# Fewer and earlier tap transfers, and half a cast moved to GpSimd, in a fused causal convolution and gated feed-forward kernel

## The chip, the cores and the metric

The kernel runs on one core of a Trainium2 chip. The core has a matrix engine (TensorE, PE in the profile), a vector engine (VectorE, DVE), an activation engine (ScalarE, ACT), a general engine (GpSimd, POOL) and SyncE (SP), which here only issues DMA transfers. POOL and ACT issue DMA transfers too. All engines run their own instruction lists in order and wait for each other by semaphores. The metric is the device time of one execution in microseconds (us); the median over several runs counts.

## The reference

`x` has shape (8, 4096, 192): 8 batches of 4096 tokens with 192 channels. `weight` is (8, 7): 8 heads of 24 channels each, 7 taps for each head. The taps of a head go through a softmax, and each channel of a token becomes the weighted sum of the last 7 tokens of its batch. The result goes through a gated feed-forward net with 1536 hidden columns.

```
w = exp(weight - max(weight)); w = w / (sum(w) + 1e-9)
y[b, s, h, g] = sum_k w[h, k] * x_pad[b, s + k, h, g]      # 6 zero tokens ahead of each batch
out = (relu(y @ w_gate) * (y @ w_val)) @ w_out
```

All inputs and the output are float32; the kernel works in float16 with float32 sums.

## The kernel before

**Units.** The tokens are cut into 16 units. A unit holds 1024 tokens of two batches, four batches apart, which are called streams; stream 0 lies on partitions 0 to 63 and stream 1 on 64 to 127 of the tile `xc` (channels in three chunks of 64, tokens along the row). `gate_val(u, w)` makes, for each of two windows of 512 tokens and each of 12 hidden blocks `f`, the gate and the value matmuls (line 530), ScalarE's relu (line 539) and VectorE's product (line 540). `project_columns` then multiplies with `Wo` (line 550) in three parts `p` = 0, 1, 2, and VectorE's `turn_out` (line 564) takes each part out of PSUM. PSUM is one ring of four double banks named `ps`, shared by all of these in program order.

**Two ways to the convolution.** For units 0 and 1 the convolution is done by TensorE with banded matrices (`conv_dense`, line 334, for unit 0 and the first window of data after it, and `conv`, line 356, whose results ScalarE copies out at line 369 and SyncE's DMA transposes bring into `xc[1]` at line 388). From unit 2 on it is done by the other engines while TensorE works on an earlier unit: `lane_load` fetches x, `lane_turn` reorders it on POOL (lines 433 and 439) and has SyncE transpose it with DMAs into the tile `x_r` (lines 434 and 441), `lane_first` (ACT, line 487), `product` (ACT, line 467), `lane_rest` (DVE, line 498 and 508) and `add` (POOL, line 476) multiply the shifted rows with the taps and add them. All of them read the tile `tap`, which has for each of 128 partitions and three chunks the 7 softmax weights of that channel's head.

**The front.** SyncE first issues five loads of float32 x (`load_raw`, line 111), in the order of the steps 1, 0, 2, 3, 4. They are cast to float16 by `cast` (line 121): steps 1, 0 and 2 on ACT, steps 3 and 4 on DVE. POOL makes a few constants (lines 141 to 160) and then issues ten loads of `w_gate` and `w_val` (`load_w`, line 208: five column slices each, cast to float16 on the way), which land on partitions 0 to 63. Copies bring each slice to partitions 64 to 127 too (`both_halves`, line 215): the first two on DVE, the next three on POOL, and the last, columns 1280 to 1535 (hidden blocks 10 and 11), by two DMAs from SyncE. POOL then loads x for `conv_dense(1)` and `conv(2)` (line 94), x for unit 2 (line 402), a 16-token head (line 413) and `Wo` (line 614).

**Taps.** ACT makes the normalized weights `wn` (line 259) on 128 partitions, 16 equal rows for each head. `load_taps` (line 283 and after) first issues the two DMAs of the last weight slice and then copies rows of `wn` to `tap`, at most 16 rows in one DMA: 32 DMAs (line 297). All of these, and the transposes after them, stand in SyncE's one list. Each DMA of SyncE takes the next of eight completion semaphores, and waits till the one eight before it has landed.

The order of the instructions is the program's own: a manual schedule, without a planner.

Of the kernel before, what the change touches and what calls it, by code (L numbers as in the profile page):

```python
# [15 lines left out]
def kernel(  # L16
# [12 lines left out]
    nc = tc.nc  # L29

    B, S, D = x.shape
    H, KW = weight.shape
    G = D // H
# [3 lines left out]
    NCH = D // 64  # L37
# [38 lines left out]
    def staged(i, j):  # L76
        return stages[i][:, XH * j : XH * (j + 1)]

    def load_x(g, streams=range(2)):
# [22 lines left out]
    xts = {0: staged(0, 0).rearrange("p (j s d) -> p j s d", s=2, d=D)}  # L102
    ROWS = [SUB + PAD, 128, 128, 128, 80]
    raw = [
        apool.tile([128, FLAT - LDVE], FP, name=f"prod{jj + 1}")[:, 0 : 2 * D] for jj in range(GSUB)
    ]
# [10 lines left out]
            ),  # L117
        )

    def cast(copy, jj):  # L120
        copy(
            out=xts[0][0 : ROWS[jj], jj, :, :].rearrange("p s d -> p (s d)"),
            in_=raw[jj][0 : ROWS[jj], :],
        )

    HR = 128 // H
# [35 lines left out]
    with nc.allow_low_precision("one of the terms is not zero"):  # L162
        nc.vector.tensor_reduce(
            out=Z[:, 112 : 112 + HR],
            in_=eye[:].rearrange("p (g i) -> p i g", i=HR),
# [4 lines left out]
        out=mask[:, :, 0],  # L170
        in_=eye[:].rearrange("p (g i) -> p g i", i=HR),
# [17 lines left out]
    for half in range(2):  # L189
        nc.tensor.matmul(  # L190
            out=raised[half][:, 0, 0 : SUB * H // 2],
# [7 lines left out]
    Wg = const.tile([128, NCH, DFF], F16)  # L199
    Wv = const.tile([128, NCH, DFF], F16)  # L200
# [4 lines left out]
    def load_w(s):  # L205
        cols = slice(CUTS[s], CUTS[s + 1])
        for src, dst in ((moe_w_gate, Wg), (moe_w_val, Wv)):
            nc.gpsimd.dma_start(
                out=dst[0:64, :, cols],
                in_=src.rearrange("(c p) f -> p c f", p=64)[:, :, cols],  # L210
            )

    def both_halves(copy, s, dst):
        cols = slice(HALVES[s], HALVES[s + 1])
        copy(out=dst[64:128, :, cols], in_=dst[0:64, :, cols])

    def pool_halves(s):
        both_halves(nc.gpsimd.tensor_copy, s, Wg)
        both_halves(nc.gpsimd.tensor_copy, s, Wv)

    for s in range(5):
        load_w(s)
    pool_halves(2)
# [6 lines left out]
        out=mx[:], in_=spread[:, 0, 0:KW], axis=mybir.AxisListType.X, op=ALU.max, negate=True  # L230
    )
    nc.scalar.activation(out=e[:, 0:KW], in_=spread[:, 0, 0:KW], func=ACTF.Exp, bias=mx[:])
    cast(nc.scalar.copy, 1)
    cast(nc.scalar.copy, 0)
    prod = const.tile([128, BW, KW], FP)
    z0 = Z[:, 112 - PAD : 113 - PAD]
    e0 = e[:, 0:1]
    nc.vector.tensor_tensor(
        out=prod[:],
# [11 lines left out]
        out=blocks[:],  # L251
# [6 lines left out]
    wn = const.tile([128, KW], FP)  # L258
    nc.scalar.activation(out=wn[:], in_=e[:, 0:KW], func=ACTF.Copy, scale=sm[:])
    cast(nc.scalar.copy, 2)  # L260

    bands = [const.tile([128, H // 2, SUB], F16, name=f"band{half}") for half in range(2)]
    for half, copy in enumerate((nc.vector.tensor_copy, nc.scalar.copy)):
        for j in range(128 // HR):
            s0 = HR * j - PAD
            lo, hi = max(0, -s0), min(BW, SUB - s0)
            nc.tensor.matmul(
                out=raised[half][:, 0, 0 : SUB * H // 2].rearrange("p (h t) -> p h t", t=SUB)[
                    :, :, s0 + lo : s0 + hi
                ],  # L270
# [7 lines left out]
            out=bands[half][:].rearrange("p h t -> p (h t)"), in_=raised[half][:, 0, 0 : SUB * H // 2]  # L278
# [4 lines left out]

    tap = const.tile([128, NCH, KW], FP)

    def load_taps():
        both_halves(nc.sync.dma_start, 5, Wg)
        both_halves(nc.sync.dma_start, 5, Wv)
        for c in range(NCH):
            r0 = 0  # L290
            while r0 < 64:
                h = (64 * c + r0) // G
                r1 = min(64, G * (h + 1) - 64 * c)
                for st in range(2):
                    for a in range(r0, r1, HR):
                        n = min(HR, r1 - a)
                        nc.sync.dma_start(  # L297
                            out=tap[64 * st + a : 64 * st + a + n, c, :],
                            in_=wn[HR * h : HR * h + n, :],
                        )  # L300
                r0 = r1

    load_taps()

    def band(h):
        return bands[h // 4][0 : SUB + PAD, h % 4, :]
# [383 lines left out]
```

## Time and profile before

| | |
|---|---|
| time, median of 3 runs | 774.67 us (773.52 to 777.39) |
| the profiled execution, its own time | 775.43 us |
| its span from first to last instruction | 773.7 us |
| TensorE busy | 763.6 us, 99% |
| VectorE busy | 669.3 us, 86% |
| ScalarE busy | 598.0 us, 77% |
| GpSimd busy | 422.5 us, 55% |
| mean granted TensorE clock | 0.998 |

A timeline row has the start in us, the length in us (of all merged instructions, if it ends with x and a number above 1), engine, line, operation and tiles; in brackets stands the idle time of that engine before the row and what ended it. "SPq" and "POOLq" are issues of DMAs; a DMA's landing time is counted from its issue. A row of the table by windows has the busy time of each engine in that stretch, the granted clock (PEclk), and the DMA traffic. In the chain of waits each row is a piece of the one chain of work that ended last.

### The profile page before, as it was taken

The numbers are of one execution on the slowest core, as the hardware profiler recorded it, in microseconds if no ns is written. First come the engines' busy times: TensorE is split into PE (matmuls) and PEld (weight loads), VectorE is DVE, ScalarE is ACT, GpSimd is POOL, SyncE is SP. The second block draws the span as 40 slices with busy tenths as digits, with TensorE's granted clock in tenths as the row PEclk, the third lists the DMA queues.
The fourth block names the chain that finished last, engine by engine and source line by source line (L and its number), as shares of the span: only waits on it lengthen the run. The fifth ranks groups of instructions, "written<-read, shape, count | busy, mean of one in ns | idle before, by whom it ended". The sixth has DMA issues, their size and how long they took to land.

```text
span 773.7 us, 21558 instructions
## 1 busy us (share of the span) xinstructions
PE 763.6 (99%) x9402; PEld 380.1 (49%) x9402; DVE 669.3 (86%) x630; ACT 598.0 (77%) x622; POOL 422.5 (55%) x190
## 2 busy tenths in 40 slices
PE   9988999999999999999999999999999999999998
PEld 4543544444444444444444444444444444444448
DVE  6858999989899898998989899898998989997691
ACT  6868787878879788797877879788797877874471
POOL 9405839368292864909458193773918548091000
PEclk9999999999999999999999999999999999999999
DMA  9934909066190842809148090651909332040402
GB/s 146 123 64 92 134 7 163 4 94 71 24 143 2 120 45 57 109 3 140 26 83 83 6 158 5 107 60 34 132 3 122 43 67 59 2 82 3 82 2 83
DMA packets 123438, 53.79 MB, mean 70 GB/s; under 512 B 87872, under 2 KB 123344, under 8 KB 123344
## 3 DMA queue, kind: packets, MB, share of 16 engines
q1 hardware_dynamic: 86416, 38.06, 30.2%
q0 software_dynamic: 36768, 14.26, 17.8%
q8 instruction: 73, 1.20, 0.7%
q14 instruction: 21, 0.17, 0.1%
q10 hardware_dynamic: 160, 0.10, 0.0%
HBM read 29.40 MB, written 25.17 MB: 71 GB/s over the span
## 4 chain that ended last, share of the span: by engine, by line
PE 91%; SPq 3%; ACT 2%; DMA 2%; issue 0%; DVE 0%
PE ps L530 61%; PE ps L550 28%; PE ps L586 2%; SPq L297 2%; ACT prod L467 1%; SPq L441 1%; DMA tap<-wn 1%; DMA prod<-in_x_dram 1%; ACT gr L539 0%; DVE hT L540 0%; DMA x_r<-x_p 0%; ACT out_s L369 0%; ACT acc L487 0%; PE ps L334 0%; SPq L111 0%
## 5 line engine op out<-in xcount | busy, mean ns | idle before, releaser
L539 ACT ACTIVATE gr<-ps 128x1024 f16<-128x1024 f32 x384 | 392.6, 1023 | 148.1 <-PE ps L530 147.7
L540 DVE TENSOR_TENSOR hT<-gr,ps 128x1024 f16<-128x1024 f16 x384 | 468.5, 1221 | 42.4 <-ACT gr L539 15.4
L476 POOL TENSOR_TENSOR prod<-prod,prod 128x1792 f32<-128x1792 f32 x70 | 278.3, 3976 | 262.9 <-DVE prod L508 226.2
L530 PE MATMUL ps<-xc,Wv 64*128 64x512 f16 x2304 | 313.0, 377 | 2.3 <-DVE out_s L564 1.7
L530 PE MATMUL ps<-xc,Wg 64*128 64x512 f16 x2304 | 313.1, 377 | 1.0 <-ACT gr L539 1.0
L550 PE MATMUL ps<-hT,Wo 128*32 128x512 f16 x4320 | 236.2, 379 | 2.2 <-DVE out_s L564 2.2
L530 PEld LDWEIGHTS <-Wv 64*128 64x128 f16 x2304 | 130.7, 94 | 121.4 <-issue 4.2
L530 PEld LDWEIGHTS <-Wg 64*128 64x128 f16 x2304 | 112.2, 94 | 139.3 <-issue 8.6
L550 PEld LDWEIGHTS <-Wo 128*32 128x32 f16 x4320 | 114.4, 97 | 122.4 <-issue 8.8
L467 ACT ACTIVATE prod<-x_r,tap 128x1024 f32<-128x1024 f16 (+1 forms) x182 | 172.8, 1037 | 0.0
L498 DVE SCALAR_TENSOR_TENSOR acc<-x_r,tap,acc 128x1024 f32<-128x1024 f16 (+1 forms) x140 | 113.9, 870 | 8.8 <-DMA xc<-out_s 8.6
L564 DVE STREAM_TRANSPOSE out_s<-ps 128x1024 f32<-128x1024 f32 x45 | 56.1, 1247 | 32.1 <-PE ps L550 32.1
L476 POOL TENSOR_TENSOR xc<-prod,prod 128x1792 f16<-128x1792 f32 x14 | 55.7, 3979 | 1.1
L439 POOL COPY x_p<-x_e 128x1536 f16<-128x1536 f16 x28 | 40.3, 1467 | 2.0 <-DMA x_e<-in_x_dram 2.0
L402 POOL DMA_DIRECT2D x_e<-in_x_dram x28 | 25.0, 900 | 4.2 <-POOL x_p L439 4.2
L487 ACT ACTIVATE acc<-x_r,tap 128x1024 f32<-128x1024 f16 (+1 forms) x28 | 21.5, 819 | 6.7 <-DMA x_r<-x_p 6.7
L498 DVE SCALAR_TENSOR_TENSOR xc<-x_r,tap,acc 128x1024 f16<-128x1024 f16 (+1 forms) x28 | 23.4, 876 | 0.0
L586 PE MATMUL ps<-Wo,hT 128*128 128x192 f16 x192 | 16.0, 246 | 0.0
L586 PEld LDWEIGHTS <-hT 128*128 128x128 f16 x192 | 15.8, 98 | 0.4 <-issue 0.4
L597 ACT COPY out_s<-ps 128x768 f32<-128x768 f32 (+2 forms) x5 | 3.2, 639 | 12.7 <-PE ps L586 12.7
L597 DVE COPY out_s<-ps 128x192 f32<-128x192 f32 x1 | 0.4, 357 | 13.3 <-PE ps L586 13.3
L508 DVE TENSOR_SCALAR prod<-x_r,tap 128x768 f32<-128x768 f16 x14 | 8.5, 610 | 0.0
(55 smaller groups left out, 61.6 us busy)
## 6 DMA issues: line engine op xcount, KB each, us to landing
out_dram<-out_s SPq DMA_DIRECT2D x63, 384.0 KB, 7.5
x_e<-in_x_dram POOLq DMA_DIRECT2D x28, 384.0 KB, 10.3
x_r<-x_p SPq DMA_TRANSPOSE x112, 3.1
out_s<-in_x_dram POOLq DMA_DIRECT2D x4, 240.0 KB, 5.9
prod<-in_x_dram SPq DMA_DIRECT2D x3, 192.0 KB
Wo<-in_moe_w_out_dram POOLq DMA_DIRECT2D x1, 576.0 KB, 10.6
out_s<-in_x_dram POOLq DMA_DIRECT2D x2, 192.0 KB, 4.1
tap<-wn SPq DMA_DIRECT2D x16, 0.4 KB, 3.4
```

Of the source, the lines that this page charges most:

```text
L402: nc.gpsimd.dma_start(out=xe[:, :, st, :, :].rearrange("p j c r -> p j (c r)"), in_=bass.AP(tensor=x.tensor, offset=x.offset + row * D, ap ...
L439: nc.gpsimd.tensor_copy(out=xp[:, :, :, st, :], in_=xe[:, :, st, :, :])
L467: nc.scalar.activation(out=prods[u, k][:, at - LDVE : at - LDVE + n], in_=shifted(u, c, k, t, n), func=ACTF.Copy, scale=tap[:, c, k : k + 1],)
L476: nc.gpsimd.tensor_tensor(out=p0[:] if k < KW - 1 else flat(u)[:, LDVE:FLAT], in0=p0[:], in1=prods.pop((u, k))[:], op=ALU.add,)
L487: nc.scalar.activation(out=accs[u][:, at : at + n], in_=shifted(u, c, 0, t, n), func=ACTF.Copy, scale=tap[:, c, 0:1],)
L498: nc.vector.scalar_tensor_tensor(out=(flat(u) if k == KW - 1 else acc)[:, at : at + n], in0=shifted(u, c, k, t, n), scalar=tap[:, c, k : k ...
L530: nc.tensor.matmul(out=pss[i][:, st, :], lhsT=W[64 * st : 64 * st + 64, c, 128 * f : 128 * (f + 1)], rhs=xcb[64 * st : 64 * st + 64, c, WI ...
L539: nc.scalar.activation(out=gr[:], in_=pss[0][:], func=ACTF.Relu)
L540: nc.vector.tensor_tensor(out=h[:, f], in0=gr[:], in1=pss[1][:], op=ALU.mult)
L550: nc.tensor.matmul(out=ps[32 * s : 32 * s + 32, b, :], lhsT=Wo[:, f, 64 * p + 32 * b : 64 * p + 32 * b + 32], rhs=hs[s // 2][:, f, s % 2, ...
L564: nc.vector.transpose(out=o[:, :, 64 * p : 64 * p + 64].rearrange("p t (b c) -> p b t c", b=2), in_=ps[:].rearrange("p b (t c) -> p b t c" ...
L586: nc.tensor.matmul(out=ps[:, i // 2, D * (i % 2) : D * (i % 2) + D], lhsT=h[:, f, st, 128 * q : 128 * (q + 1)], rhs=Wo[:, f, :], start=(f ...
```

## The change

The code of three places differs; the order of everything else is the same.

1. The taps are sent in 20 DMAs instead of 32. One DMA covers all rows of a chunk that belong to one head in one stream (8, 16 or 24 rows), and reads 8 rows of `wn`, each of them one, two or three times by a step of zero.
2. The 14 DMAs of the chunks 0 and 1 stand in SyncE's list ahead of the two DMAs of the last weight slice; the 6 of chunk 2 stand behind them.
3. The cast of x step 1 is split: GpSimd casts the first 192 of the 384 columns before it issues the ten weight loads, and ACT casts the other 192.

```diff
-    def cast(copy, jj):
+    def cast(copy, jj, lo=0, hi=2 * D):
         copy(
-            out=xts[0][0 : ROWS[jj], jj, :, :].rearrange("p s d -> p (s d)"),
-            in_=raw[jj][0 : ROWS[jj], :],
+            out=xts[0][0 : ROWS[jj], jj, :, :].rearrange("p s d -> p (s d)")[:, lo:hi],
+            in_=raw[jj][0 : ROWS[jj], lo:hi],
         )
...
+    cast(nc.gpsimd.tensor_copy, 1, 0, D)
     for s in range(5):
         load_w(s)
...
-    cast(nc.scalar.copy, 1)
+    cast(nc.scalar.copy, 1, D)
     cast(nc.scalar.copy, 0)
...
-    def load_taps():
-        both_halves(nc.sync.dma_start, 5, Wg)
-        both_halves(nc.sync.dma_start, 5, Wv)
-        for c in range(NCH):
-            r0 = 0
-            while r0 < 64:
-                h = (64 * c + r0) // G
-                r1 = min(64, G * (h + 1) - 64 * c)
-                for st in range(2):
-                    for a in range(r0, r1, HR):
-                        n = min(HR, r1 - a)
-                        nc.sync.dma_start(
-                            out=tap[64 * st + a : 64 * st + a + n, c, :],
-                            in_=wn[HR * h : HR * h + n, :],
-                        )
-                r0 = r1
-
-    load_taps()
+    for c in range(NCH):
+        r0 = 0
+        while r0 < 64:
+            h = (64 * c + r0) // G
+            r1 = min(64, G * (h + 1) - 64 * c)
+            row = wn[HR * h : HR * h + 8, :]
+            for st in range(2):
+                nc.sync.dma_start(
+                    out=tap[64 * st + r0 : 64 * st + r1, c, :],
+                    in_=bass.AP(
+                        tensor=row.tensor,
+                        offset=row.offset,
+                        ap=[row.ap[0], [0, (r1 - r0) // 8], [1, KW]],
+                    ),
+                )
+            r0 = r1
+        if c == 1:
+            both_halves(nc.sync.dma_start, 5, Wg)
+            both_halves(nc.sync.dma_start, 5, Wv)
```

## The prediction

> **What bounds the kernel now.** I read the table by windows first, then TensorE's timeline, then the chain of waits backwards. The table says that TensorE is the bound, and where it is not.
>
> ```profile
> 42.50:62.60 20.10, 17.87 (x308) 9.41 (x306) 11.41 (x13) 13.41 (x22) 0.00 (x0) 1.00 0.27 58
> 62.60:75.00 12.40, 9.33 (x74) 4.10 (x72) 8.89 (x11) 9.62 (x11) 7.63 (x4) 0.86 0.53 100
> 75.00:100.00 25.00, 25.00 (x246) 13.03 (x246) 23.59 (x20) 19.87 (x20) 22.46 (x10) 1.00 0.91 123
> ```
>
> The second number is TensorE's busy time, the second last but one the granted clock. From 75 us on TensorE is busy all the time at full clock. Between 42.5 and 75 it loses 5.3 us, and in the second stretch the clock drops to 0.86. Its timeline shows both:
>
> ```profile
> 9.30 0.39 PE L530 MATMUL ps<-xc,Wg 64*128 64x512 f16 x2
> ...
> 23.55 0.82 PE L530 MATMUL ps<-xc,Wg 64*128 64x512 f16 x6
> ...
> 57.30 5.36 PE L550 MATMUL ps<-hT,Wo 128*32 128x512 f16 x96 [2.23 <-DVE out_s L564]
> 62.60 0.82 PE L530 MATMUL ps<-xc,Wg 64*128 64x512 f16 x6
> ...
> 66.45 0.82 PE L530 MATMUL ps<-xc,Wv 64*128 64x512 f16 x6 [1.74 <-DVE out_s L564]
> 68.24 0.89 PE L530 MATMUL ps<-xc,Wg 64*128 64x512 f16 x6 [0.96 <-ACT gr L539]
> 69.49 1.47 PE L530 MATMUL ps<-xc,Wv 64*128 64x512 f16 x6 [0.37 <-DVE hT L540]
> 70.73 1.51 PE L530 MATMUL ps<-xc,Wg 64*128 64x512 f16 x6
> 72.01 0.96 PE L530 MATMUL ps<-xc,Wv 64*128 64x512 f16 x6
> 72.80 0.82 PE L530 MATMUL ps<-xc,Wg 64*128 64x512 f16 x6
> 73.44 0.82 PE L530 MATMUL ps<-xc,Wv 64*128 64x512 f16 x6
> ```
>
> The brackets are waits: 2.23 + 1.74 + 0.96 + 0.37 = 5.30 us. Behind them three groups of six matmuls take 72.80 - 69.49 = 3.31 us, where a group normally takes 73.44 - 72.80 = 0.64: 1.39 us lost to the clock. So the place is worth 5.3 + 1.4 = 6.7 us in all. The gap of 2.23 by itself cost no clock: the window that holds it has 1.00.
>
> The waits name VectorE's take-out (line 564) and ScalarE's relu (line 539). Both only come late because those engines began the work for unit 2 late:
>
> ```profile
> 52.81 3.27 DVE L498 SCALAR_TENSOR_TENSOR acc<-x_r,tap,acc 128x1024 f32<-128x1024 f16 x4 [8.62 <-DMA xc<-out_s]
> ```
>
> ```profile
> 3.52 1.06 ACT L121 CAST out_s<-prod 128x384 f16<-128x384 f32 x2
> 4.49 0.29 ACT L259 ACTIVATE wn<-e,sm 128x7 f32<-128x7 f32 x1
> ...
> 43.15 2.00 ACT L369 CAST out_s<-ps 112x480 f16<-112x480 f32 x5 [0.20 <-PE ps L356]
> 51.63 1.55 ACT L487 ACTIVATE acc<-x_r,tap 128x1024 f32<-128x1024 f16 x2 [6.49 <-DMA x_r<-x_p]
> ...
> 60.52 6.76 ACT L467 ACTIVATE prod<-x_r,tap 128x768 f32<-128x768 f16 x7
> 67.17 3.02 ACT L539 ACTIVATE gr<-ps 128x1024 f16<-128x1024 f32 x3
> ```
>
> ScalarE was free at 45.15 and stood till `x_r` landed at 51.63; VectorE's first step needs ScalarE's `acc`, so the DMA that its bracket names is not what ended its wait. `x_r` comes through SyncE's list:
>
> ```profile
> 13.83 0.72 SPq L215 DMA_DIRECT2D Wg<-Wg  x1
> ...
> 15.77 22.00 SPq L297 DMA_DIRECT2D tap<-wn  x32
> ...
> 39.18 11.33 SPq L441 DMA_TRANSPOSE x_r<-x_p  x8
> ...
> 86.19 12.04 SPq L441 DMA_TRANSPOSE x_r<-x_p  x8
> ```
>
> The 32 tap DMAs hold SyncE till 37.8 with no pause. What the transposes read was made much earlier:
>
> ```profile
> 1.88 0.41 POOL L160 MEMSET prod<- 6x384 f32 x1
> 2.25 0.83 POOL L208 DMA_DIRECT2D Wg<-in_moe_w_gate_dram  x1
> ...
> 19.96 0.56 POOL L413 DMA_DIRECT2D head<-in_x_dram  x1
> ...
> 28.07 0.62 POOL L433 COPY turned<-head 16x192 f16<-16x192 f16 x2 [6.50 <-DMA head<-in_x_dram]
> 28.64 2.87 POOL L439 COPY x_p<-x_e 128x1536 f16<-128x1536 f16 x2
> ```
>
> `x_p` is ready at 31.5; its first transpose goes out at 39.18, 7.7 us later, for the taps alone.
>
> **The taps.** Single issues, from the chain:
>
> ```profile
> 17.21 0.52 SPq L297
> 17.78 0.66 SPq L297
> ```
>
> 8 rows take 0.52, 16 rows 0.66, each with 0.04 to 0.06 between. For 24 rows no row exists: the low end is 0.52 (the size costs nothing), the high end 0.80 (the same step once more). I take the mean of all 32, 22.00 / 32 = 0.69, which lies between. The first tap waits for `wn`, 4.49 + 0.29 = 4.8. Fourteen taps end at 4.8 + 9.6 = 14.4 (by the ends with their gaps 12.7 and 16.7). The first copy of the last weight slice went out at 13.83 when its load had landed:
>
> ```profile
> Wg<-in_moe_w_gate_dram POOLq DMA_DIRECT2D x1, 240.0 KB, 6.4
> ...
> Wg<-Wg SPq DMA_DIRECT2D x1, 96.0 KB, 5.4
> ```
>
> That load goes out later by the delay of the weight issues (below, 1.4), so the copies go out at about 15.3 and 16.1, whichever of the two is last. Landing 5.4 later gives 20.7 and some 21.5 for the second, of which no landing is shown; block 10 begins at 23.55. This cover is about 2 us; without it each us costs TensorE a us. Behind them six taps end at 16.8 + 6 x 0.69 = 21.
>
> **What is late next.** SyncE now waits for POOL. POOL's whole list moves by the cast and its wait, 1.4 us, so `x_p` is ready at 31.5 + 1.4 = 32.9. Eight transposes took 11.33 in a quiet stretch (before) and 12.04 beside x loads (at 86 us); the x loads of line 94 will now run beside them, so I take 12.04. The last one began landing at 50.51 and had landed at 51.63: 1.1. `x_r` is there at 32.9 + 12.0 + 1.1 = 46.0 instead of 51.63. ScalarE is free at 45.15 plus the shift of the front (0.6, below). From line 487 to the first relu it took 67.17 - 51.63 = 15.5 us; now 46.0 + 15.5 = 61.5. Without the first wait TensorE finishes the first gate group at 62.60 + 0.82 - 2.23 + 0.6 = 61.8. So ScalarE isn't late, and there are 0.3 us to spare, plus about as much in the buffers behind. VectorE begins 1.2 after ScalarE, at 47.2, and reaches its first take-out 3.2 later, at 50.4; TensorE's third part, which waited for it, can start at 57.30 - 2.23 + 0.6 = 55.7. The take-out lasts about 1.2, so this slack is some 4 us. Gain: the whole 5.3, and with it the 1.4 of the clock.
>
> **The cast on GpSimd.** POOL is ready at 1.88 + 0.41 = 2.3 and now waits for x step 1. When that lands no row says; not later than 3.52, where ScalarE's cast starts without a wait. The cast of 192 columns: the copies of 192 columns at 28.07 take 0.31 each. The first weight load goes out between 2.3 + 0.3 = 2.6 and 3.52 + 0.35 = 3.9 instead of 2.25, a delay of 0.35 to 1.6; I take 1.4, as the row of ScalarE is the only one near. ScalarE's halved cast saves 0.25 us of its 0.53, which only moves `wn` by 0.1, since it waits for VectorE's sum; I count nothing.
>
> The delay reaches TensorE through VectorE's list:
>
> ```profile
> 8.25 0.27 DVE L215 COPY Wv<-Wv 64x384 f16<-64x384 f16 x1
> 8.55 0.69 DVE L344 CAST xc<-ps 128x512 f16<-128x512 f32 x1
> ```
>
> ```profile
> Wv<-in_moe_w_val_dram POOLq DMA_DIRECT2D x1, 48.0 KB, 3.4
> ```
>
> The fourth weight load lands 3.4 after its issue at 4.32, so at 7.7, and its copy at 8.25 had 0.5 to spare. Behind that copy stands the cast of chunk 1, which releases the matmuls at 9.30. A delay of 1.4 less 0.5 is 0.9 for them. Against it, the x loads have less beside them. The ends: 0.3 gained (VectorE could cast step 3 earlier, as ScalarE and VectorE wait for x there), 1.6 lost (all of the delay). I take 0.6. Later slices have more room than the 1.4.
>
> The Trainium skill has a rule against this cast ("SBUF — State Buffer", section "SBUF: two separate sides"): a GpSimd operation and a VectorE operation with two inputs in SBUF exclude each other for the whole instruction. Here VectorE's small operations of the softmax run just when POOL would cast. By it the cast could begin some 0.3 later and the sum would be 0.3 higher, as an estimate; no run yet shows it, and I leave it out of the sum.
>
> **The sum.** Against the profiled execution, 775.43 us: -5.3 (waits) - 1.4 (clock) + 0.6 (front) = -6.1, so 769.3. That execution lies 0.76 above the median of 774.67; the same change from the median gives 768.6. A measurement here can tell about 0.5%, 3.9 us, from no change: faster is below 770.8, slower above 778.5.
>
> **The rivals.**
>
> First, `x_r` comes late again, though less. From 46.5 on, each us costs one. If the head that POOL waits for lands later than shifted (it took from 19.96 to 28.07 beside other loads), or the transposes take longer among the x loads, `x_r` at 48 to 50 costs 1.5 to 3.5, and part of the clock's 1.4: 770.3 to 773.5. For it: the transposes lose their quiet stretch. Against: SyncE then has nothing else to issue.
>
> Second, slower: the tap DMAs hold the last weight slice. Each tap waits for the one eight before it to land, so slow landings add up ahead of the copies. Place: TensorE at 23.55, block 10. TensorE stalls from an issue at 15.3 + 2 = 17.3 on, us for us, and the clock's 1.4 comes with a long gap. The whole gain of 6.1 is gone with a stall of 4.7, which is an issue at 22; over 3.9 slower is an issue at 26, time 779 and above. For that 14 taps would have to take 21 us, 1.5 each. The 32 of before took 0.69 each with the same rule of eight, though at an emptier time in part. A stall of 2 to 4 us would give 772 to 774.
>
> Third, nothing happens: `x_r` stays at 51 because something else in its way (landing of the loads, the eight semaphores) takes the place of the taps; then 774.5 to 775.5. Against it stands `x_p` at 31.5.
>
> **How the numbers follow.** Forecast as described, with 766.9 to 770.6 by the ends of the front: 0.66. `x_r` late in part: 0.17, of which 0.06 is still faster by over 0.5%. Taps hold the weight slice: 0.10, of which half is slower by over 0.5%. Nothing happens: 0.05. Something else that makes it slower: 0.02. So faster 0.72, same 0.21 (0.11 + 0.05 + 0.05), slower 0.07. The range 767.2 to 773.0 leaves out the slower cases, no change, the stalls above 773 and a little at the low end, together some 0.19.
>
> **What would show it.** In the profile after: SyncE's taps begin at 4.8, the slice's copies go out near 15.3, SyncE stands till about 30 and its eight transposes start near 33. ScalarE's bracket ahead of line 487 falls from 6.49 to about 0.3, and TensorE has no bracket of line 564 after 50 us and a clock of 1.00 from 62 to 75. The matmuls at 9.30 move to about 9.9, and the first weight load goes out near 3.6. The prediction is wrong if block 10 gets a bracket, if `x_r` lands after 48, or if the front loses over 1.6.

## The result, and the profile after

The changed kernel takes 770.94 us in the median of 6 runs (768.82 to 771.82), the kernel before 774.5 us in the same session. The ratio, which goes by the means, is 0.9947, with a 95% interval of 0.9927 to 0.9967: faster by 0.5%. The profiled execution took 771.82 us, the slowest of the six, against 775.43 us before; the traces differ by 3.61 us.

The table by windows of the changed kernel, over the same stretches as in the prediction. Line numbers are those of each kernel's own file: line 532 here is line 530 before.

```profile
42.50:62.60 20.10, 20.10 (x328) 10.09 (x326) 15.56 (x18) 17.29 (x26) 0.00 (x0) 1.00 0.25 52
62.60:75.00 12.40, 11.00 (x102) 5.47 (x98) 9.93 (x10) 10.15 (x12) 10.08 (x5) 1.00 0.65 118
```

The 5.3 us of waits have shrunk to 1.4, and the clock is 1.00 in both rows. TensorE's timeline shows what is left there, and a new wait ahead of it:

```profile
9.64 0.39 PE L532 MATMUL ps<-xc,Wg 64*128 64x512 f16 x2 [1.01 <-DVE xc L346]
...
22.63 0.63 PE L336 MATMUL ps<-band,out_s 118*32 118x112 f16 x38 [0.94 <-DMA out_s<-in_x_dram]
23.20 0.82 PE L532 MATMUL ps<-xc,Wg 64*128 64x512 f16 x6
...
63.10 0.81 PE L532 MATMUL ps<-xc,Wg 64*128 64x512 f16 x6
63.92 0.82 PE L532 MATMUL ps<-xc,Wv 64*128 64x512 f16 x6
65.71 0.82 PE L532 MATMUL ps<-xc,Wg 64*128 64x512 f16 x6 [0.96 <-ACT gr L541]
66.97 0.82 PE L532 MATMUL ps<-xc,Wv 64*128 64x512 f16 x6 [0.43 <-DVE hT L542]
```

The matmuls of chunk 1 come at 9.64 instead of 9.30. The convolution of the first window of unit 1 then waits for its x (line 94), so that the group which began at 21.58 before begins at 23.20: the front has lost 1.62 us. Later ScalarE's relu is late again, by less. The account of the trace: -5.30 (waits of before) + 0.96 + 0.43 + 0.17 (the gap between 63.10 and 63.92 is 0.82 where 0.65 is normal) - 1.4 (clock) + 1.62 = -3.5, near the 3.61 seen.

SyncE's list does what the edit says, and then waits for GpSimd:

```profile
4.74 10.22 SPq L294 DMA_DIRECT2D tap<-wn  x14
15.08 0.72 SPq L215 DMA_DIRECT2D Wg<-Wg  x1
15.98 0.64 SPq L215 DMA_DIRECT2D Wv<-Wv  x1
16.68 4.40 SPq L294 DMA_DIRECT2D tap<-wn  x6
32.39 1.22 SPq L436 DMA_TRANSPOSE x_r<-turned  x1
35.21 10.79 SPq L443 DMA_TRANSPOSE x_r<-x_p  x8
```

It is free from 21.1 on; the transposes start at 35.21, not 39.18. GpSimd's timeline shows why not sooner:

```profile
3.44 0.47 POOL L121 CAST out_s<-prod 128x192 f16<-128x192 f32 x1 [1.15 <-DMA prod<-in_x_dram]
3.86 0.83 POOL L208 DMA_DIRECT2D Wg<-in_moe_w_gate_dram  x1
...
11.30 0.82 POOL L215 COPY Wg<-Wg 64x768 f16<-64x768 f16 x1 [0.97 <-DMA Wg<-in_moe_w_gate_dram]
...
15.01 1.78 POOL L94 DMA_DIRECT2D out_s<-in_x_dram  x2
...
22.44 0.57 POOL L415 DMA_DIRECT2D head<-in_x_dram  x1
...
31.74 0.62 POOL L435 COPY turned<-head 16x192 f16<-16x192 f16 x2 [7.68 <-DMA head<-in_x_dram]
32.32 2.87 POOL L441 COPY x_p<-x_e 128x1536 f16<-128x1536 f16 x2
```

The cast waits 1.15 us for x and shifts the weight issues by 1.6 (3.86 instead of 2.25). A wait of 0.97 for the third weight slice follows, so the x loads of line 94 go out 2.5 us later than before (15.01 against 12.53), the head lands 3.7 later (31.74 against 28.07), and `x_p` is ready at 35.2 instead of 31.5. ScalarE's row shows the effect:

```profile
44.77 2.00 ACT L371 CAST out_s<-ps 112x480 f16<-112x480 f32 x5 [0.21 <-PE ps L358]
49.10 1.55 ACT L489 ACTIVATE acc<-x_r,tap 128x1024 f32<-128x1024 f16 x2 [2.33 <-DMA x_r<-x_p]
```

By the chain of waits the last transpose lands at 48.8, and ScalarE starts on `x_r` at 49.1, 2.5 us earlier than before and 3.1 later than forecast.

### The profile page after: what moved, and what is told of

The parts are those of the page before. It is cut to its first block, busy times and chain, and to the rows that moved or that the text cites. A ratio compares the mean times of both kernels' runs of the same rounds, so it can differ in the third digit from the quotient of the medians.

```text
span 770.1 us, 21550 instructions
## 1 busy us (share of the span) xinstructions
PE 761.8 (99%) x9402; PEld 380.9 (49%) x9402; DVE 669.9 (87%) x630; ACT 598.1 (78%) x622; POOL 423.1 (55%) x191
## 4 chain that ended last, share of the span: by engine, by line
PE 91%; POOL 3%; ACT 2%; DMA 1%; issue 1%; SPq 1%; DVE 0%; ACTq 0%; POOLq 0%
PE ps L532 60%; PE ps L552 28%; PE ps L588 2%; ACT prod L469 1%; SPq L443 1%; DMA Wg<-in_moe_w_gate_dram 1%; DMA x_r<-x_p 1%; POOL out_s L94 0%; POOL Wg L215 0%; POOL Wv L215 0%; POOL x_p L441 0%; DMA prod<-in_x_dram 0%; POOL x_e L404 0%; ACT out_s L371 0%; ACT acc L489 0%
## 5 line engine op out<-in xcount | busy, mean ns | idle before, releaser
L566 DVE STREAM_TRANSPOSE out_s<-ps 128x1024 f32<-128x1024 f32 x45 | 56.1, 1247 | 30.9 <-PE ps L552 30.8
```

What stands on the lines that cost most here:

```text
L566: nc.vector.transpose(out=o[:, :, 64 * p : 64 * p + 64].rearrange("p t (b c) -> p b t c", b=2), in_=ps[:].rearrange("p b (t c) -> p b t c" ...
```

## The experiments

The theory to test first (A): the taps gave what the prediction said, and GpSimd's wait and cast took the missing 2.5 us by shifting its list. Its rival (B): the 14 early taps, which now run beside the weight loads, slow those loads; the 0.97 us wait for the third slice is theirs. The four runs of the first group take the two parts of the change one by one.

**The early taps without the cast.**

```diff
-    cast(nc.gpsimd.tensor_copy, 1, 0, D)
...
-    cast(nc.scalar.copy, 1, D)
+    cast(nc.scalar.copy, 1)
```

> The changed kernel without the GpSimd cast (ScalarE casts all of x step 1, as before); 20 taps, 14 of them early. Theory A (the wait and the cast on GpSimd shift its whole list, and that took the missing 2.5 us): x_p ready near 31.5 as before, conv_dense(1) waits for no x, x_r ready at 43.5 to 46, TensorE loses neither the 5.3 us of waits nor the clock's 1.4: 6.2 to 6.9 us faster than before, about 768. Theory B (the 14 early taps slow the weight loads that run beside them): GpSimd still waits about 1 us for weight slice 2, x_p at 32.5 or later, a front some 0.5 to 1 us longer: 5 to 5.5 us faster, about 769.3.

Measured: 770.19 us in the median (768.25 to 770.81), before 774.49; ratio 0.9936 (0.9919 to 0.9953). Its profiled execution was the fastest of the six, 768.25, and shows what full success looks like: no wait of TensorE after 13 us, and ScalarE goes from one line to the next without a pause:

```profile
43.11 2.00 ACT L370 CAST out_s<-ps 112x480 f16<-112x480 f32 x5 [0.21 <-PE ps L357]
44.97 1.59 ACT L488 ACTIVATE acc<-x_r,tap 128x1024 f32<-128x1024 f16 x2
```

The six times fall in two groups: two at 768.25 and 768.5, four at 770.0 to 770.8. So even without the cast the full gain comes in some executions only. Neither theory had that. What puts an execution into one group or the other is seen in the traces of single executions only, one for each kernel.

**The cast alone, on the kernel before.**

```diff
+    cast(nc.gpsimd.tensor_copy, 1, 0, D)
     for s in range(5):
         load_w(s)
...
-    cast(nc.scalar.copy, 1)
+    cast(nc.scalar.copy, 1, D)
```

> The kernel before with only the GpSimd cast; 32 taps behind the weight slice. Theory A: weight loads 1.6 us later, GpSimd waits for slice 2, x for conv_dense(1) arrives late: TensorE's front 1 to 1.6 us longer; x_p near 35, still hidden behind the taps till 37.8, so x_r as before. 0.8 to 1.8 us slower than before, about 776. Theory B: without early taps the wait for slice 2 goes; the front loses only the 0.3 us at the first gate matmuls: 0 to 0.5 us slower.

Measured: 778.4 us, ratio 1.0045 (1.003 to 1.0059): slower by some 3.9 us in the medians, more than twice the upper end of theory A (0.8 to 1.8), and nothing of theory B. What I had missed is in SyncE's and TensorE's rows:

```profile
15.09 0.73 SPq L215 DMA_DIRECT2D Wg<-Wg  x1
16.26 0.60 SPq L215 DMA_DIRECT2D Wv<-Wv  x1
16.98 23.75 SPq L298 DMA_DIRECT2D tap<-wn  x32
40.84 1.21 SPq L435 DMA_TRANSPOSE x_r<-turned  x1
42.16 12.55 SPq L442 DMA_TRANSPOSE x_r<-x_p  x8
```

```profile
50.05 5.36 PE L551 MATMUL ps<-hT,Wo 128*32 128x512 f16 x96
...
61.50 7.33 PE L551 MATMUL ps<-hT,Wo 128*32 128x512 f16 x96 [6.08 <-DVE out_s L565]
```

In the kernel before, the taps stand behind the copies of the last weight slice, which wait for its load. Later weight issues move the copies, all taps and the transposes: those start at 42.16 instead of 39.18, and TensorE waits 6.08 us where it waited 2.23. The matmuls behind that gap take 7.33 instead of 5.36. The shift of the copies, 1.2 us, is less than half of what `x_r` loses:

```profile
55.83 1.55 ACT L488 ACTIVATE acc<-x_r,tap 128x1024 f32<-128x1024 f16 x2 [10.34 <-DMA x_r<-x_p]
```

ScalarE starts on it 4.2 us later than before (51.63). The taps themselves take 23.75 us instead of 22.00, since SyncE waits 2.0 us among them for earlier taps to land, where it waited 0.2 before; and the transposes take 1.2 us longer to the landing. The six times lie within 1 us, so the whole loss comes with the cast; how it lengthens the taps and the transposes is not shown. The shift itself goes through SyncE, and in the changed kernel this path is cut by the fewer taps.

**The cast, with all 20 taps behind the weight slice; and the 20 late taps without the cast.** The first moves the two copies ahead of the loop over chunks; the second also leaves the cast to ScalarE.

```diff
+    both_halves(nc.sync.dma_start, 5, Wg)
+    both_halves(nc.sync.dma_start, 5, Wv)
     for c in range(NCH):
...
-        if c == 1:
-            both_halves(nc.sync.dma_start, 5, Wg)
-            both_halves(nc.sync.dma_start, 5, Wv)
```

> The changed kernel with all 20 taps behind the two copies of the last weight slice; the GpSimd cast stays. 20 taps at 0.73 end near 31, before x_p. Theory A: the same time as the changed kernel, 771 (within 0.7), with GpSimd's 1 us wait for slice 2 still there. Theory B: that wait goes, x_p is ready near 34, the front loses only 0.4: 769 to 769.7.

> The kernel before with 20 taps instead of 32, all behind the weight slice, and no GpSimd cast: only the number of taps is changed. The taps end near 15.8 + 20 x 0.73 = 30.4, before x_p at 31.5, so by both theories the taps are off the path: x_r at 43.5 to 46, full gain of 6.2 to 6.9 us, about 768. If e1 is slower than this by over 0.5 us, the early place of the taps costs something (theory B).

Measured: with the cast 770.88 us, ratio 0.9948 (0.9933 to 0.9963); without it 769.93 (768.21 to 770.6), ratio 0.993 (0.9915 to 0.9946). Against the early taps (770.94 and 770.19) the place of the taps makes no difference: sending fewer of them is what counts. That speaks against theory B. So does GpSimd's row of the late taps without a cast:

```profile
11.41 1.14 POOL L215 COPY Wg<-Wg 64x1152 f16<-64x1152 f16 x1 [1.07 <-DMA Wg<-in_moe_w_gate_dram]
```

Up to this point that kernel's instructions are those of the kernel before, where the same copy began at 10.35 without a wait. Over all slices, GpSimd waits 0.25 to 0.97 us in the four traces that have the cast ahead of the weight loads, and from none to 1.07 in the seven that have no cast. So a wait of up to 1 us comes and goes between executions with the same instructions ahead of it; neither the taps nor the cast are needed for it. Theory A holds for the cast's part, 0.75 to 0.95 us (770.94 - 770.19 and 770.88 - 769.93; the intervals of either pair overlap, but both pairs point the same way), but not for the rest: 20 taps alone gain 4.3 to 4.6, not 6.2 to 6.9.

The new theory (C): with the taps out of the way, GpSimd's list decides when `x_r` is there, and the landing of the head ends it. It had no slack: `x_p` must be ready by about 32 for `x_r` at 46. Its rival (D): the transposes got slower because they now run beside the x loads of `load_x(3)`; from the first issue to the landing of the last it took 12.4 us before, 13.6 in the changed kernel and 13.5 with late taps and cast.

**The loads for unit 2 issued first**, without the cast and with it:

```diff
-    xts[2] = load_x(2)
     lane_load(2)
+    xts[2] = load_x(2)
```

> The 20 taps of the changed kernel without the GpSimd cast (as e1_early_taps_alone), and the loads of x and of the head for unit 2 are issued ahead of the x load for conv(2) instead of behind it. Theory C (with the taps out of the way, GpSimd's list up to x_p decides when x_r is there, and the landing of the head ends it): the head goes out some 1.8 us earlier and lands 2 to 4 us earlier, x_p near 29.5, x_r by 44, ScalarE without a wait in line 488: all runs near 768.0, none at 770 and above. Theory D (x_r is late because the transposes run beside the x loads of load_x(3), 13.5 us instead of 12.4): x_p earlier moves the loads with it; the 1.1 us stay, but x_r is earlier too: 768 to 769.

> The changed kernel, with its GpSimd cast, and the loads for unit 2 ahead of the x load for conv(2). Theory C: x_p near 31 to 32, x_r by 45.5, no wait in line 489; what is left of the cast's price is the first gate matmuls, 0.4 us, plus whatever conv_dense(1) waits for its x: 768.4 to 769.4. If it stays at 771, the price of the cast doesn't go through x_r at all.

Measured, in a session whose kernel before was slower (776.39): 768.64 us (767.84 to 768.74), ratio 0.9896 (0.9874 to 0.9917), without the cast; 769.48 with it (five runs of 768.59 to 769.85 and one of 772.79), ratio 0.9914 (0.9889 to 0.9939). None of the six without the cast reaches 769: the slower group of times is gone. GpSimd's rows without the cast:

```profile
18.73 0.54 POOL L414 DMA_DIRECT2D head<-in_x_dram  x1
...
27.37 0.62 POOL L434 COPY turned<-head 16x192 f16<-16x192 f16 x2 [5.32 <-DMA head<-in_x_dram]
27.94 2.87 POOL L440 COPY x_p<-x_e 128x1536 f16<-128x1536 f16 x2
```

`x_p` is ready at 30.8, and ScalarE doesn't wait. With the cast the part through `x_r` is gone as well, and some 0.8 us of the cast's price remain, all in the front, where its trace shows waits at the first matmuls of chunk 1 and for the x of line 94:

```profile
9.60 0.39 PE L532 MATMUL ps<-xc,Wg 64*128 64x512 f16 x2 [1.06 <-DVE xc L346]
...
22.18 0.63 PE L336 MATMUL ps<-band,out_s 118*32 118x112 f16 x38 [0.47 <-DMA out_s<-in_x_dram]
```

**`load_x(3)` ahead of the copies, alone and with the other move:**

```diff
+        if u == 0:
+            xts[3] = load_x(3)
         if u + 2 < NUNIT:
             lane_turn(u + 2)
-        if u == 0:
-            xts[3] = load_x(3)
```

> As e1_early_taps_alone, but GpSimd issues the x loads of load_x(3) ahead of the copies for unit 2, in the time in which it waits for the head, so that they are over before the transposes. Theory D: the eight transposes and the landing of the last take 12.4 us instead of 12.2 to 13.8, x_r about 1 us earlier: near 769.2 in the median. Theory C alone: no change, 770.2. Later head (more loads in the queues) would make it slower.

> Both moves on the kernel of e1_early_taps_alone: loads for unit 2 first, and load_x(3) ahead of the copies. By both theories x_r is there before 44 and ScalarE doesn't wait: 767.8 to 768.3 in all runs, the full 6.7 us of the place. Slower than e5 would mean that the x loads now hold the head back.

Measured, in the session of the loads-first kernels: alone 770.44 us (768.32 to 771.65), the wide spread of the early taps alone (770.19). Its profiled execution, a fast one, issued the eight transposes in 11.51 us, with GpSimd's loads beside them only at the start; that is no less than the 10.51 of the early taps alone, which had the x loads beside them. Theory D falls by the traces: with the cast alone it took 13.65 us from the first issue of the transposes to the landing of the last, though nothing of GpSimd's DMA queue ran beside them, and with the early taps alone at most 12.3, though the x loads did. With both moves 768.41 (768.12 to 768.82), not to be told from the loads-first kernel. The two kernels of this pair differ by the move of the loads for unit 2 alone, and with it the spread is gone.

**Are these two waits one behind the other?** The same move of the loads on the kernel before, with its 32 taps:

> The kernel before with one edit: the loads for unit 2 ahead of the x load for conv(2). The 32 taps stay as they were. If the taps and GpSimd's list are two waits one behind the other, x_p near 29 is no use while SyncE sends taps till 37.8: the time of before, within 0.5 us either way. A gain of over 2 us would mean that the landing of the loads, not the taps, set x_r in the kernel before.

Measured: 774.7 us (12 runs), before 774.58; ratio 0.9996 (0.998 to 1.0012). `x_p` was ready at 29.5, and yet:

```profile
17.22 22.34 SPq L297 DMA_DIRECT2D tap<-wn  x32
39.67 1.20 SPq L434 DMA_TRANSPOSE x_r<-turned  x1
40.98 10.85 SPq L441 DMA_TRANSPOSE x_r<-x_p  x8
```

So the taps alone bind there, and GpSimd's list only once they are fewer. TensorE's rows behind the same place show something else that I had overlooked:

```profile
67.78 0.82 PE L530 MATMUL ps<-xc,Wv 64*128 64x512 f16 x6 [1.75 <-DVE out_s L564]
69.56 0.82 PE L530 MATMUL ps<-xc,Wg 64*128 64x512 f16 x6 [0.96 <-ACT gr L539]
70.81 0.82 PE L530 MATMUL ps<-xc,Wv 64*128 64x512 f16 x6 [0.43 <-DVE hT L540]
71.46 0.83 PE L530 MATMUL ps<-xc,Wg 64*128 64x512 f16 x6
```

The waits are nearly those of the kernel before (1.74, 0.96, 0.37), but a group takes 0.65 us from start to start, and the granted clock from 62.6 to 75 is 1.00 instead of 0.86. So the 1.4 us of the clock in the forecast belong to the one execution that was profiled, and not to each one with these waits.

**Is the cast's price the wait, or the cast?** On the kernel with the cast and the loads first, the cast stands behind the first four weight loads:

```diff
-    cast(nc.gpsimd.tensor_copy, 1, 0, D)
     for s in range(5):
+        if s == 2:
+            cast(nc.gpsimd.tensor_copy, 1, 0, D)
         load_w(s)
```

> As e6_cast_lane_load_first, but GpSimd's cast stands behind the first four weight loads (issued till 4.9) instead of ahead of all. If the price of the cast is GpSimd's wait for x ahead of the weight loads, there is no wait any more and only the cast's own 0.4 us for the later slices: no wait for the cast of chunk 1 at the first gate matmuls, 768.4 to 768.9, some 0.8 us under e6. If the price is the cast itself (an engine's port, a slower cast beside VectorE), it stays at 769.3 to 769.8.

Measured: 768.53 us (768.14 to 768.92), ratio 0.991 (0.9893 to 0.9928), before 774.58. GpSimd's rows:

```profile
4.95 0.35 POOL L121 CAST out_s<-prod 128x192 f16<-128x192 f32 x1
5.25 0.64 POOL L208 DMA_DIRECT2D Wg<-in_moe_w_gate_dram  x1
```

No wait, and 0.35 us for the cast. The median is 0.95 us below the one with the cast in front, but the two ran in different sessions, and their ratios (0.991 and 0.9914) don't tell them apart. TensorE's row is clearer:

```profile
9.93 0.39 PE L533 MATMUL ps<-xc,Wg 64*128 64x512 f16 x2
```

The wait of 1.06 at the first matmuls of chunk 1 is gone, and so is the one for the x of line 94. So what the cast costs in the front is, by these traces, GpSimd's wait for x ahead of the weight loads and not the cast. The cast gains nothing either: 768.64 without it, 768.53 with it. Both, and the kernel with both moves, are near 768.5, faster than both kernels of the case.

## Why the prediction was right or wrong

Forecast: 768.6 us, range 767.2 to 773.0, faster. Measured: 770.94, faster. The direction was right, and so was the cause of the gain: the 32 taps held the transposes, and fewer of them free `x_r` earlier. But the gain was 3.56 us instead of 6.1, and what happened is not the main case (chance 0.66) but the first rival, `x_r` late in part (chance 0.17, 770.3 to 773.5). Two of the three signs that were to show the forecast wrong came: `x_r` landed after 48 (48.8), and the front lost over 1.6 (1.62). The range held because it took in this rival.

770.94 lies just above the 770.8 below which the forecast saw a gain that can be told from none; the interval of the six runs tells it all the same. Of the 2.5 us that the trace is above its forecast (771.82 against 769.3), 1.56 are what TensorE still lost to the late `x_r`, and 1.0 is the front (1.62 lost where 0.6 was counted).

- **The place and its worth, 5.3 + 1.4 us: the waits right, the clock only for one execution.** The kernels in which ScalarE doesn't wait, and no cast stands ahead of the weight loads, reach 768.4 to 768.6, 6.0 to 8.0 us under the kernel before in their sessions (774.58 and 776.39). The clock's 1.4 went in the changed kernel although waits of 0.96 and 0.43 stayed. But it isn't in every execution of the kernel before: of 17 in the last session, 6 show a mean granted clock of 1.000 (774.2 to 774.6 us), 8 the 0.998 of the profiled one (774.1 to 776.3). Taking the whole 1.4 from the median was more than the runs bear out.
- **The taps: right.** 10.22 / 14 = 0.73 each against the 0.69 taken, which was the mean of all 32 with their waits; the weight slice's copies went out at 15.08 and 15.98, forecast 15.3 and 16.1. Block 10 got no wait. That SyncE would then wait for POOL was right too. That 14 of them go early brought nothing: late taps give the same time.
- **"POOL's whole list moves by the cast and its wait, 1.4 us": wrong, and this is the step that failed.** The first issue moved by 1.6, but the list up to `x_p` by 3.7, since a wait of 0.97 for a weight slice and a later landing of the head (9.3 us after its issue, not 8.1) came on top. I had taken the one trace of before as the list's fixed length. There it was hidden behind the taps, and nothing in the time showed how it varies: without any cast, `x_p` was ready at 32.7 and 33.7 in two traces, where I had counted on 31.5.
- **`x_r` at 46.0: wrong by 3.1**, of which 2.3 is the step above (`x_p` at 35.2 instead of 32.9); the transposes and their landing took 13.6 and not 13.1, and ScalarE started 0.3 behind the landing. Why the transposes vary, from 11.9 (32 taps, loads first) to 13.65 (cast alone), isn't settled; the x loads beside them don't explain it.
- **ScalarE's spare time: too small in the forecast.** It was 2.33 late and TensorE lost 0.96 + 0.43 + 0.17 = 1.56, so some 0.8 were free; I had counted 0.3 and about as much behind it.
- **The front, 0.6 lost: 0.34 at the first gate matmuls as described**, since x landed earlier (VectorE's casts of steps 3 and 4 ended at 6.9, not 7.6). "Later slices have more room than the 1.4" left out the x of line 94, which stands in the same list: 0.94 of wait, 1.62 lost by 23.2 us in the profiled execution. Over all runs the cast costs 0.75 to 0.95. The spread "766.9 to 770.6 by the ends of the front" doesn't follow from these ends: 0.3 gained and 1.6 lost give 767.7 and 769.6.
- **The rivals.** The first is what happened, in most executions. The tap DMAs did not hold the weight slice. The other side came true only for the cast alone, which no rival had: it is slower by 3.9 us on the kernel before.
- **The cast beside VectorE.** VectorE's two-input operation ran from 3.39 to 3.71 in the changed kernel, the cast from 3.44 to 3.91. In the four traces with the cast ahead of the weight loads, GpSimd's next instruction starts 0.15 to 0.16 us behind the end of that operation, whether the cast starts at 3.44 or at 3.59. From the cast's start to the next instruction it is 0.42 us in the changed kernel and 0.30 with the cast behind four weight loads, a price of 0.12 and not the 0.3 estimated. The Trainium skill's rule ("SBUF — State Buffer", "SBUF: two separate sides") would let the cast start only after VectorE's two-input operation. The rows agree with it as far as they go, since spans on GpSimd are rough.

## What to carry to other kernels

When a queue is cleared out of the way, the work that had been hidden behind it becomes the path, and its length in one trace is a sample, not a constant: ask how much it varies and give it slack by issuing its loads first (here two swapped lines, which took the slower group of times away). An instruction that waits for a DMA, put at the head of an engine's list, moves all that the engine issues later; behind the issues that others need, the same cast cost nothing that the runs show. What one trace shows lost to the clock needn't be lost in the next execution. Fewer transfers mattered, their earlier place did not.

## What the runs showed of the hardware that I had not expected

A weight load's landing varies by about 1 us between executions with the same instructions ahead of it: the third slice let GpSimd's copy begin at 10.40 without a wait in the loads-first kernel with the cast and at 11.30 in the changed kernel, the fourth at 10.35 before and at 11.41 with late taps alone. The head landed 5.9 to 8.6 us after its issue with the loads of unit 2 first, and 7.8 to 9.3 with them second. That these two make the two groups of times is likely but not shown: the fast execution of the early taps alone waited 0.76 us for the fourth slice too.

A small DMA of 8 to 24 rows of 28 bytes costs SyncE about the same: 0.69 us each for 32 of 8 or 16 rows, 0.73 for 14 of 8 to 24 rows, 0.77 to 0.82 for 20 of these behind the weight slice, waits among them included.

A gap of 6.08 us on TensorE was followed by matmuls that took 1.97 us longer, while gaps of 3.34, of 2.23, and of 0.96 and 0.43 cost no clock. Three gaps of 1.74, 0.96 and 0.37 us cost 1.4 us in the kernel before, and gaps of 1.75, 0.96 and 0.43 in its loads-first form cost none.
